# Chunk mask as extra contraction rows of the scores, attention output with queries on partitions, feed-forward transposed and spread between head pairs

## The chip, the cores and the metric

The kernel runs on one core of one Trainium2 chip. The metric is the device time of one execution in microseconds (us); the median of several runs is quoted.

Five engines work side by side, each on its own queue of instructions (in the kernel before TensorE is busy for 77% of the span and VectorE for 74%): TensorE (PE in the profile; PEld is its weight load), VectorE (DVE), ScalarE (ACT), GpSimd (POOL) and SyncE (SP). A matmul has a stationary operand (`lhsT`, loaded as weights: the page counts 2292 loads for the 2292 matmuls) and a moving one (`rhs`). Its cost is counted below in *columns* of the moving operand.

## The reference

Attention in which a query sees only its best 6 chunks of 32 keys, then a gated feed-forward. B=4, H=8, S=768, D=64; the feed-forward has width 512, and two halves of 512.

```python
k_min, k_max = k_chunks.min(axis=3), k_chunks.max(axis=3)             # per chunk of 32 keys
ub = sum(max(q * k_min, q * k_max), axis=-1)                          # bound of each chunk
top_chunks = argsort(where(causal_by_chunk, ub, -1e9))[..., -6:]
scores = where(chunk_selected & causal, q @ k.T / sqrt(D), -1e9)
x = softmax(scores) @ v                                               # heads side by side: B, S, 512
h = relu(x @ w_in); u, v = h[..., :512], h[..., 512:]
gated = u * (w_spatial @ layernorm(v) + b_spatial)                    # w_spatial mixes positions
out = gated @ w_out
```

## The kernel before

For each batch, for each of four head pairs: bounds and chunk selection (`sel_phase`), then scores and attention output (`score_phase`). After the four pairs, the feed-forward of that batch. The parts that matter (cuts marked with `...`):

```python
def score_phase(hi):
    ho = hi * D
    for gi, (q0, q1) in enumerate(qg_bounds):            # queries 0..511, 512..767
        av_ps = pst2([D + 1, 512])                       # head dim on partitions, plus the row of sums
        ...
        for t in range(t_last + 1):                      # key tiles of 128
            sc_ps = psum.tile([P, 512], F32, tag="sc", name="sc", bufs=2)
            mm(sc_ps[:, :Wv], lhsT=kT[ho:ho + D, t * P:(t + 1) * P],           # 64 rows
               rhs=qT[ho:ho + D, q0 + qoff:q1], start=True, stop=False)
            mm(sc_ps[:, :Wv], lhsT=expandM[:, t * P:(t + 1) * P],              # 24 rows: chunk mask
               rhs=selT[hi][:, q0 + qoff:q1], start=False, stop=True)
            if q0 + qoff <= t * P < q1:
                nc.vector.tensor_add(sc_ps[:, d0:d0 + P], sc_ps[:, d0:d0 + P], diagT)
            nc.scalar.activation(out=exp16[:, :Wv], in_=sc_ps[:, :Wv], func=Act.Exp, scale=scale)
            ...
        for t in range(t_last + 1):
            mm(av_ps[:, qoff:qoff + Wv], lhsT=v16[:, t, hi, :], rhs=exp16L[t][:, :Wv],   # 128 rows
               start=(t == 0), stop=(t == t_last))
        nc.vector.reciprocal(recip[:, :W], av_ps[D:D + 1, :W])                 # one partition, 512 columns
        nc.gpsimd.partition_broadcast(recip_bc_t[:, :W], recip[:, :W])
        nc.vector.tensor_mul(...)                                              # into xT
```

The weights, with the spatial matrix and its 36 transposes, are loaded before the first pair. The inputs come as float32 and are cast by ScalarE.

The softmax here doesn't subtract the row's maximum and nothing guards it: scores larger than these inputs give would overflow.

## Time and profile before

| | before |
|---|---|
| median | 689.34 us (687.81 to 690.26, 4 runs) |
| TensorE / VectorE / ScalarE busy | 529.4 / 508.3 / 224.2 us |
| one head pair | 31.3 us (mask matmuls of two neighbouring pairs start at 239.1 and 270.4 us) |

The page's first two parts, of the kernel before: busy time of each engine with its share of the span, and the span in 40 slices (tenths of busy; PEclk is the clock granted to TensorE in tenths).

```profile
PE 529.4 (77%) x2292; PEld 206.6 (30%) x2292; DVE 508.3 (74%) x1653; ACT 224.2 (33%) x464; POOL 50.2 (7%) x90
...
PE   0179797789778787969796877877976889796977
...
DVE  0177787877887778777977778786787877787686
...
PEclk9999999999885555555896555555688555555599
```

Neither TensorE nor VectorE is full, and neither has an idle stage. The clock is at half (5) in the attention of the second to fourth batch. The 9s of the first ten slices are not a measurement: the first record of the clock in this trace comes at 168.2 us, and what precedes it is shown as 1.0 (and counts as 1.0 in every mean clock quoted below, unless the text says that it is corrected). That TensorE was at half speed there too is seen from the spacing of its matmuls, in the timeline of the kernel before (start in us, duration in us, engine, line, operation, output and inputs, `partitions x elements`):

```profile
52.28 0.42 PE L195 MATMUL aps_454<-exp_471,v_253 128*65 128x256 f16 x1
52.63 0.39 PE L182 MATMUL sc<-qT,kT 64*128 64x256 f16 x1
52.95 0.39 PE L184 MATMUL sc<-selT_300,expandM 24*128 24x256 f16 x1
53.28 0.32 PE L195 MATMUL aps_454<-exp_477,v_253 128*65 128x128 f16 x1
...
58.04 0.42 PE L195 MATMUL aps_488<-exp_507,v_253 128*65 128x256 f16 x1
58.25 0.42 PE L195 MATMUL aps_488<-exp_513,v_253 128*65 128x256 f16 x1
...
172.22 0.38 PE L222 MATMUL sc<-w_in_sb,xT 128*128 128x512 f16 x1
172.44 0.38 PE L223 MATMUL aps_1772<-w_in_sb,xT 128*128 128x512 f16 x1
```

Read starts, not durations: durations overlap. Two attention-value matmuls of 256 columns start 0.21 us apart (58.04, 58.25); two feed-forward matmuls of 512 columns start 0.22 apart (172.22, 172.44). So the attention runs at half the rate per column. And L182 to L184, also 256 columns, takes 0.32: there is a gap of 0.11 us where the contraction goes from 64 rows to 24, and another where it goes on to 128. The records of the weight loads (PEld) fit a load that is not hidden: the loads of L182 and L184 start with their own matmuls (at 52.63 and 52.95 us, each 0.10 us long), while between the feed-forward matmuls, all of 128 rows, the load starts one matmul ahead (at 172.22 us for the matmul of 172.44).

The reciprocal of one row of 512 sums takes 3.35 us, and a diagonal mask add stands in the queue behind such a reciprocal. (This add then waited for its own matmul as well. Elsewhere the reciprocal alone holds it: one runs from 260.17 to 263.52 us, the matmul of the add behind it ends at 263.02, and the add starts at 263.56.) In the list of what each line waits for, the exponentials (L190) show the consequence: in all they waited 236.9 us for those adds (columns: releaser, us in total, times).

```profile
  DVE sc L188: 236.9, 134
  PE sc L184: 54.8, 99
```

The chain that ended last, kernel before:

```profile
PE 62%; DVE 22%; ACT 5%; issue 5%; DMA 3%; POOL 3%; DVEq 0%; POOLq 0%; ACTq 0%; SPq 0%
```

### The profile page before, as it was taken

How to read it: one execution, taken by the hardware profiler on the slowest of the kernel's cores; microseconds unless marked ns; L12 is line 12 of the kernel's file. 1: busy time of each engine (PE TensorE's matmuls, PEld its weight loads, DVE VectorE, ACT ScalarE, POOL GpSimd, SP SyncE). 2: the span in 40 equal slices, each digit the busy share in tenths (PEclk: the TensorE clock that was granted, in tenths of full speed). 3: DMA queues.
4: the chain of work that ended last, by engine and by line, in shares of the span. 5: the costliest groups of instructions: out<-in, count | busy, mean ns of one | idle time of the engine just before them, and what ended most of it. 6: DMA issues, size and time to landing. Idle time of an engine off the chain costs nothing.

```text
span 688.0 us, 7728 instructions
## 1 busy us (share of the span) xinstructions
PE 529.4 (77%) x2292; PEld 206.6 (30%) x2292; DVE 508.3 (74%) x1653; ACT 224.2 (33%) x464; POOL 50.2 (7%) x90
## 2 busy tenths in 40 slices
PE   0179797789778787969796877877976889796977
PEld 0133333223333233323333232322333333332333
DVE  0177787877887778777977778786787877787686
ACT  3135262423125233433205434343202524251310
POOL 4000010101000100001000101010000000010100
PEclk9999999999885555555896555555688555555599
DMA  9992121201041121210123110000001000000002
GB/s 198 209 211 47 30 46 44 58 2 30 0 139 32 44 46 30 46 30 0 29 77 82 26 29 23 7 7 0 7 22 71 0 7 1 7 0 6 5 2 93
DMA packets 83162, 29.99 MB, mean 44 GB/s; under 512 B 76208, under 2 KB 79536, under 8 KB 83120
## 3 DMA queue, kind: packets, MB, share of 16 engines
q1 hardware_dynamic: 81280, 26.75, 17.2%
q0 software_dynamic: 1840, 2.75, 2.2%
q8 instruction: 18, 0.29, 0.2%
q14 instruction: 24, 0.20, 0.1%
HBM read 24.38 MB, written 6.29 MB: 45 GB/s over the span
## 4 chain that ended last, share of the span: by engine, by line
PE 62%; DVE 22%; ACT 5%; issue 5%; DMA 3%; POOL 3%; DVEq 0%; POOLq 0%; ACTq 0%; SPq 0%
PE sc L184 15%; PE sc L182 12%; PE sc L245 5%; DVE selb L162 4%; DVE recip L198 4%; PE sc L222 3%; DMA ws_raw<-in_moe_w_spatial_dram 2%; POOL recip_bc_t L200 2%; DVE av_tmp L206 2%; PE aps L149 1%; DVE sc L188 1%; DVE ub_sb L152 1%; DVE stats L230 1%; PE aps L125 1%; PE aps L253 1%
## 5 line engine op out<-in xcount | busy, mean ns | idle before, releaser
L182 PE MATMUL sc<-qT,kT 64*128 64x256 f16 (+1 forms) x320 | 124.0, 396 | 28.6 <-ACT exp_1653 L190 1.4
L188 DVE TENSOR_TENSOR sc<-sc,diagT 128x128 f32<-128x128 f32 x192 | 53.8, 295 | 59.4 <-PE sc L184 47.6
L200 POOL PARTITION_BROADCAST recip_bc_t<-recip x64 | 43.0, 672 | 593.3 <-DVE recip L198 576.0
L167 PE MATMUL aps<-identity,selb 128*24 128x128 f16 x192 | 35.8, 276 | 44.5 <-DVE selb L162 39.6
L245 PE MATMUL sc<-vn_sb,wsT 128*128 128x512 f16 x144 | 47.4, 447 | 14.6 <-DVE vn_sb L239 14.6
L184 PEld LDWEIGHTS <-expandM 24*128 24x128 f16 x320 | 32.0, 100 | 88.1 <-issue 77.5
L182 PEld LDWEIGHTS <-kT 64*128 64x128 f16 x320 | 30.8, 100 | 87.2 <-issue 82.4
L222 PE MATMUL sc<-w_in_sb,xT 128*128 128x512 f16 x96 | 38.7, 440 | 0.0
L149 PE MATMUL aps<-kmaxP,qposF 64*128 64x24 f16 x192 | 22.1, 185 | 19.3 <-DVE ub_sb L152 12.5
L167 PEld LDWEIGHTS <-selb 128*24 128x24 f16 x192 | 17.9, 94 | 57.6 <-DVE selb L162 46.1
L97 PE MATMUL aps<-identity,ws_raw 128*128 128x128 f16 x36 | 5.3, 269 | 31.4 <-DMA ws_raw<-in_moe_w_spatial_dram 31.4
L98 DVE COPY wsT<-aps 128x128 f16<-128x128 f16 x36 | 5.3, 219 | 30.6 <-PE aps L97 30.6
L144 ACT ACTIVATE qposF<-qT 64x768 f16<-64x768 f16 x32 | 26.8, 836 | 0.4
L145 ACT ACTIVATE qnegNF<-qT 64x768 f16<-64x768 f16 x32 | 26.6, 831 | 0.2
L245 PEld LDWEIGHTS <-wsT 128*128 128x128 f16 x144 | 15.5, 109 | 34.4 <-issue 26.3
L149 PEld LDWEIGHTS <-qposF 64*128 64x128 f16 x192 | 14.1, 103 | 38.2 <-issue 29.3
L255 DVE COPY gT_sb<-aps 128x128 f16<-128x128 f16 x96 | 18.9, 218 | 7.9 <-PE aps L253 3.6
L234 ACT ACTIVATE rstd<-mv,eps_t 128x1 f32<-128x1 f32 x24 | 7.1, 294 | 52.4 <-DVE mv L232 52.4
L248 DVE SCALAR_TENSOR_TENSOR gated<-sc,u_sb 128x512 f16<-128x512 f32 x24 | 16.2, 688 | 10.1 <-PE sc L245 9.8
L150 PE MATMUL aps<-kminN,qnegNF 64*128 64x24 f16 x192 | 20.6, 178 | 1.8 <-ACT qnegNF L145 1.8
L126 DVE COPY qT<-aps 128x128 f16<-128x128 f16 x96 | 20.4, 212 | 1.9 <-PE aps L125 1.8
L123 DVE COPY kT<-aps 128x128 f16<-128x128 f16 x96 | 20.4, 213 | 0.1
(1506 smaller groups left out, 1150.7 us busy)
## 6 DMA issues: line engine op xcount, KB each, us to landing
out_dram<-out_sb SPq DMA_DIRECT2D x24, 256.0 KB, 2.0
ws_raw<-in_moe_w_spatial_dram POOLq DMA_DIRECT2D x1, 1152.0 KB, 16.2
w_in_sb<-in_moe_w_in_dram POOLq DMA_DIRECT2D x1, 1024.0 KB, 9.4
xT<-av_tmp SPq DMA_DIRECT2D x16, 64.0 KB, 1.9
w_out_sb<-in_moe_w_out_dram POOLq DMA_DIRECT2D x1, 512.0 KB, 10.9
xT<-av_tmp SPq DMA_DIRECT2D x16, 32.0 KB, 1.8
kp_242<-in_k_dram SPq DMA_DIRECT2D x2, 192.0 KB, 3.1
qp_243<-in_q_dram SPq DMA_DIRECT2D x2, 192.0 KB, 3.5
```

Of the source, the lines that this page charges most:

```text
L144: nc.scalar.activation(qpos, qT_h, func=Act.Relu)
L145: nc.scalar.activation(qnegN, qT_h, func=Act.Relu, scale=-1.0)
L149: mm(ub_ps, lhsT=qpos[:, qi * P:(qi + 1) * P], rhs=kmax, start=True, stop=False)
L162: nc.vector.tensor_scalar(selb, in0=ub_sbL[qi], scalar1=max8L[qi][:, TOPK - 1:TOPK], scalar2=NEG, op0=Alu.is_lt, op1=Alu.mult)
L167: nc.tensor.transpose(stp, selbL[qi], identity)
L182: mm(sc_ps[:, :Wv], lhsT=kT[ho:ho + D, t * P:(t + 1) * P], rhs=qT[ho:ho + D, q0 + qoff:q1], start=True, stop=False)
L184: mm(sc_ps[:, :Wv], lhsT=expandM[:, t * P:(t + 1) * P], rhs=selT[hi][:, q0 + qoff:q1], start=False, stop=True)
L188: nc.vector.tensor_add(sc_ps[:, d0:d0 + P], sc_ps[:, d0:d0 + P], diagT)
L198: nc.vector.reciprocal(recip[:, :W], av_ps[D:D + 1, :W])
L200: nc.gpsimd.partition_broadcast(recip_bc_t[:, :W], recip[:, :W])
L222: mm(hu, lhsT=lhsT, rhs=w_in_sb[:, ko, 0:DH], start=(ko == 0), stop=(ko == NDO - 1))
L245: mm(vs_ps, lhsT=wsT[:, si, ti * P:(ti + 1) * P], rhs=vn_sb[:, si, :], start=(si == 0), stop=(si == NQT - 1))
```

## The change

The intent: (1) put the chunk mask into the same matmul as the scores, by giving keys and queries 64 more rows that hold chunk membership and the selection flags, so that every contraction has 128 rows and the separate mask matmuls go; (2) compute the attention output with queries on partitions, so that the sums are a column and six reciprocals per partition suffice; (3) do the diagonal mask as a matmul of an identity with a triangle; (4) transpose six tiles into one PSUM tile and move them out with one instruction of 768 columns; (5) cast in the loads, issued by GpSimd; (6) compute the feed-forward transposed where that saves transposes, and place its pieces between the head pairs of the next batch.

The core of the diff (most of it cut):

```diff
-                        mm(sc_ps[:, :Wv], lhsT=kT[ho:ho + D, t * P:(t + 1) * P], rhs=qT[ho:ho + D, q0 + qoff:q1],
-                           start=True, stop=False)
-                        mm(sc_ps[:, :Wv], lhsT=expandM[:, t * P:(t + 1) * P], rhs=selT[hi][:, q0 + qoff:q1],
-                           start=False, stop=True)
-                        if q0 + qoff <= t * P < q1:
-                            nc.vector.tensor_add(sc_ps[:, d0:d0 + P], sc_ps[:, d0:d0 + P], diagT)
+                    mm(sc[:, col:col + n], lhsT=kh[hi][:, t * P:(t + 1) * P], rhs=a[hi][:, q0:q0 + n],
+                       start=True, stop=not dg)                       # 128 rows: 64 data, 64 mask
+                    if dg:
+                        mm(sc[:, col:col + P], lhsT=identity, rhs=tri, start=False, stop=True)
...
-                        mm(av_ps[:, qoff:qoff + Wv], lhsT=v16[:, t, hi, :], rhs=exp16L[t][:, :Wv], ...)
-                    nc.vector.reciprocal(recip[:, :W], av_ps[D:D + 1, :W])
-                    nc.gpsimd.partition_broadcast(recip_bc_t[:, :W], recip[:, :W])
+                    mm(avv[:, qi, :], lhsT=e[:, c:c + P], rhs=vt[:, t, hi, 0:D + 1],
+                       start=(t == 0), stop=(t == qi))
+            nc.vector.reciprocal(rec, avv[:, :, D:D + 1])             # 128 partitions, 6 columns
...
+            nc.gpsimd.tensor_tensor(km[:, m], in0=kmm[:, m:m + 1, :]..., in1=hmask..., op=Alu.mult)
...
+    load(0); load(1); load_weights(); prep(0)                         # (four lines)
+    for i in range(NPAIR):
+        if i + 2 < NPAIR: load(i + 2)
+        if i + 1 < NPAIR: prep(i + 1)
+        attend(i)
+        if i == 1: prep_weights()
+        ...                                                           # after the 4th pair: todo = mlp(b);
+            todo.pop(0)()                                             # else a share of the pieces
```

## The prediction

> **What bounds it now.** No engine is full: the page's busy shares are TensorE 77%, VectorE 74%, ScalarE 33%. The chain of waits is 62% TensorE, 22% VectorE, with the two score matmuls (queries times keys, then mask expansion) 27% of the span. The attention of a head pair takes about 31 us, the feed-forward of a batch about 36 us (group start times), in series; the first 36.5 us wait for the spatial weights.
>
> TensorE is slow there for two reasons, read in the timeline. A 256-column score matmul starts 0.325 us after the one before it, while attention-value matmuls of that width follow each other at 0.213: contraction rows switch between 64, 24 and 128, and each switch exposes about 0.11 us of weight load. And 0.213 us for 256 columns is half speed: feed-forward matmuls of 512 columns run at 0.216. The clock reads 0.50 in the attention after 202 us; the 1.00 before 178 us precedes the first record, and the spacings there contradict it. [...]
>
> **What changes.** Columns streamed per pair fall from 19,776 to 13,962 (mask matmuls and mask transposes go; attention-value 65 columns wide with 128 rows stationary; diagonal mask as an identity matmul added). Feed-forward stays at 58,368 per batch. In all 461,000 columns: 192 us at the fast clock, 385 at the slow. Every matmul has 128 contraction rows, so I expect loads hidden.
>
> VectorE (estimates from durations of before): per pair two reductions 1.9 us, two clamps 1.5, ten max 0.9, mask arithmetic 0.5, three 768-wide copies 2.5 (128-wide copies start 0.133 apart), normalisation 1.3: about 8.7. The 1x512 reciprocals (3.35 us each), the 192 diagonal adds (54 us) and small copies go. Feed-forward about 12.5 per batch. Sum about 195 against 508. ScalarE: exponentials of 1024 columns about 1.0 us; about 155 in all. GpSimd: 96 casting loads at about 1 us (weight loads: 0.8 to 1.06).
>
> **On the critical path.** Start: GpSimd is free at 9.4 us (as before), builds masks, first keys land near 22 us, scores near 33. Four pairs without feed-forward at about 13 us: 52. Twelve pairs with a quarter of a feed-forward each: TensorE 11.9 us fast, VectorE 12, ScalarE 10, coupled by two-deep PSUM buffers: about 16.5 each, 198. The last feed-forward stands alone: about 29. Sum about 312 us.
>
> **Predicted: 312 us, 8 in 10 between 268 and 372.** Faster by over 2%: 0.98; within 2%: 0.01; slower: 0.01.
>
> **What would show it.** First transposes near 22 us; granted clock mostly 1.0 in the middle, mixed in the first four pairs; score matmuls of 512 columns spaced near 0.22 us without load gaps; VectorE near 195 us busy; no engine over 85%; final stage of about 29 us with VectorE and ScalarE partly idle.
>
> **What would make it wrong.** If half clock holds through the middle, TensorE needs 24 us a pair and the time is near 400. If the two accumulator banks, shared by bounds, attention-value and feed-forward, make TensorE wait in order, pairs take 20 us (about 355). If the 128-byte casting loads land late, or the key-bound product on GpSimd queues behind loads, every pair waits. If all overlap well, pairs take 13.5 and the time is 270.

The kernel before shows this much: its feed-forward matmuls of 512 columns start 0.427 us apart from 163.8 us on and 0.216 us apart from 168.8 us on, after 5 us of them without a pause. So the full clock in the middle was the author's estimate. 33 to the first scores, 52 for four pairs, 198 for twelve and 29 for the end make 312 us. The landing of the first keys at 22 us and the first scores at 33 are estimates too, of which only GpSimd's start at 9.4 us was measured (9.35 in the kernel before). ScalarE's 1.0 us for 1024 columns is an estimate near what 0.485 us for 384 and 0.597 for 512 in the kernel before give (1.04). The first record of the clock, of 1.0, starts at 168.2 us and ends at 178.4; the prediction's 178 is its end.

## More of the kernel before

VectorE timeline, kernel before:

```profile
247.71 3.35 DVE L198 RECIPROCAL recip<-aps_2641 1x512 f32<-1x512 f32 x1 [0.94 <-PE aps_2641 L195]
251.49 0.30 DVE L188 TENSOR_TENSOR sc<-sc,diagT 128x128 f32<-128x128 f32 x1 [0.43 <-PE sc L184]
```

## The result, and the profile after

| | before | after |
|---|---|---|
| median | 689.34 us (4 runs) | 290.94 us (289.23 to 292.39, 4 runs) |
| ratio of fast runs | | 0.422 (95% interval 0.4203 to 0.4236) |
| TensorE / VectorE / ScalarE busy, us | 529.4 / 508.3 / 224.2 | 222.4 / 170.7 / 154.3 |

Ratios are the mean time of one kernel's fast runs over that of the other's fast runs of the same rounds, so they are not quite the ratio of the medians. Executions over 1.5% slower than the fastest of the same kernel are left out of the means.

Page, kernel after, first two parts:

```profile
PE 222.4 (77%) x2340; PEld 144.9 (50%) x2340; DVE 170.7 (59%) x498; ACT 154.3 (54%) x217; POOL 98.1 (34%) x150
...
PE   0037028787879798989798989978888989799994
...
DVE  8337005888788875565579865474688654238330
...
PEclk9999758999999999999999999999999999999999
```

The busy share of TensorE is 77% as before, and says nothing by itself: by the shapes in the traces it streamed 554,496 columns in 529.4 us busy before, 1.0 per ns, and now 461,472 in 222.4, 2.1 per ns. The clock is 1.0 from about 46 us to the end. TensorE stands still from about 29 to 40 us (fifth and sixth slice); we come back to that.

Timeline of TensorE, kernel after:

```profile
68.49 0.38 PE L213 MATMUL sc<-a_693,kh_0_92 128*128 128x512 f16 x1
68.70 0.22 PE L216 MATMUL sc<-tri,identity 128*128 128x128 f16 x1
68.76 0.38 PE L213 MATMUL sc<-a_693,kh_0_92 128*128 128x512 f16 x1
```

512 columns now take 0.21 us and the diagonal 0.06, with no gap although the stationary operand changes each time: the load of the next one starts with the matmul before it (the identity's at 68.49 us for 68.70, that of `kh` at 68.70 for 68.76).

Busy time by stage, kernel after: pairs without feed-forward (57 to 87 us), and two stretches of 60 us with it. Columns are the stretch, its length, then busy time and instructions of PE, PEld, DVE, ACT, POOL, then the clock, the DMA share and GB/s.

```profile
57.00:87.00 30.00, 24.56 (x373) 18.67 (x372) 24.51 (x78) 20.84 (x25) 18.00 (x27) 1.00 1.02 66
93.00:153.00 60.00, 52.87 (x573) 34.44 (x572) 38.88 (x117) 38.51 (x55) 21.31 (x32) 1.00 0.70 67
153.00:213.00 60.00, 53.39 (x577) 34.64 (x575) 39.60 (x119) 38.06 (x55) 18.89 (x28) 1.00 0.60 61
```

With feed-forward TensorE is busy 88 to 89%, VectorE about 65%. Without it TensorE and VectorE are level at 82%. The chain that ended last:

```profile
PE 50%; ACT 23%; DMA 8%; POOL 7%; DVE 7%; issue 3%; ACTq 0%; DVEq 0%; POOLq 0%
```

VectorE, 22% of the chain before, has fallen to 7%. ScalarE has risen from 5 to 23%, over half of it (13%) the exponentials: TensorE heads the chain, but ScalarE comes next, not VectorE.

### The profile page after: what moved, and what is told of

The parts are those of the page before. It is cut to its first block, busy times and chain, and to the rows that moved or that the text cites. A ratio compares the mean times of both kernels' runs of the same rounds, so it can differ in the third digit from the quotient of the medians.

```text
span 287.5 us, 5812 instructions
## 1 busy us (share of the span) xinstructions
PE 222.4 (77%) x2340; PEld 144.9 (50%) x2340; DVE 170.7 (59%) x498; ACT 154.3 (54%) x217; POOL 98.1 (34%) x150
## 4 chain that ended last, share of the span: by engine, by line
PE 50%; ACT 23%; DMA 8%; POOL 7%; DVE 7%; issue 3%; ACTq 0%; DVEq 0%; POOLq 0%
ACT e L217 13%; PE acc L322 11%; PE sc L213 7%; PE acc L310 7%; DMA w_out_sb<-in_moe_w_out_dram 6%; PE acc L224 5%; PE acc L333 5%; PE acc L285 5%; DVE stats L289 2%; PE tr L234 2%; POOL kp L140 2%; PE sc L216 2%; DMA out_dram<-o 2%; ACT uT L312 2%; PE acc L324 2%
## 5 line engine op out<-in xcount | busy, mean ns | idle before, releaser
L217 ACT ACTIVATE e<-sc 128x1024 f16<-128x1024 f32 (+1 forms) x96 | 84.0, 916 | 44.0 <-PE sc L216 42.9
L140 POOL DMA_DIRECT2D kp<-in_k_dram x32 | 26.7, 839 | 54.1 <-PE tr L152 48.0
L224 PEld LDWEIGHTS <-e 128*128 128x128 f16 x672 | 27.0, 98 | 31.3 <-ACT e L217 17.8
L216 PE MATMUL sc<-tri,identity 128*128 128x128 f16 x192 | 39.5, 222 | 0.0
L322 PE MATMUL acc<-wsT,vn 128*128 128x512 f16 (+1 forms) x192 | 37.2, 325 | 0.4 <-ACT uT L312 0.2
L322 PEld LDWEIGHTS <-vn 128*128 128x128 f16 x192 | 18.2, 98 | 12.2 <-issue 1.1
L310 PE MATMUL acc<-xT,w_in_sb 128*128 128x512 f16 (+1 forms) x128 | 23.4, 325 | 0.9 <-ACT uT L312 0.7
L333 PE MATMUL acc<-w_out_sb,gT 128*128 128x512 f16 x96 | 23.1, 378 | 0.4 <-ACT o L336 0.3
L216 PEld LDWEIGHTS <-identity 128*128 128x128 f16 x192 | 19.0, 99 | 7.4 <-issue 5.7
L285 PE MATMUL acc<-w_in_sb,xT 128*128 128x512 f16 x96 | 22.2, 379 | 0.0
L152 PE MATMUL tr<-identity,kp 128*128 128x128 f16 x96 | 10.0, 229 | 14.7 <-DMA kp<-in_k_dram 14.6
L180 DVE TENSOR_TENSOR acc<-acc,cmask 128x40 f32<-128x40 f32 x16 | 3.3, 208 | 25.6 <-PE acc L177 22.7
L161 POOL TENSOR_TENSOR km<-kmm,hmask 128x48 f16<-128x48 f16 x32 | 8.3, 276 | 26.3 <-DVE kmm L155 22.6
```

The lines of the kernel that those rows point to most:

```text
L140: nc.gpsimd.dma_start(out=kp[:, :, hi, :], in_=view(k))
L216: mm(sc[:, col:col + P], lhsT=identity, rhs=tri, start=False, stop=True)
L217: nc.scalar.activation(out=e[:, BASES[g]:BASES[g] + WIDTHS[g]], in_=sc[:, 0:WIDTHS[g]], func=Act.Exp, scale=scale)
L224: mm(avv[:, qi, :], lhsT=e[:, c:c + P], rhs=vt[:, t, hi, 0:D + 1], start=(t == 0), stop=(t == qi))
L285: mm(hv, lhsT=x[:, ko, bi * P:(bi + 1) * P], rhs=w_in_sb[:, ko, DH:DFF], start=(ko == 0), stop=(ko == NDO - 1))
L310: mm(hu[:, 0:t1 - t0], lhsT=w_in_sb[:, ko, db * P:(db + 1) * P], rhs=x[:, ko, t0:t1], start=(ko == 0), stop=(ko == NDO - 1))
```

## The experiments

Twelve kernels were run, in four groups; those of a group ran on the same chip. The first asks what each part of the change is worth, from the changed kernel; the second loosens one limit at a time in the kernel before; the third (b_both, km_late, best) and the fourth (mask_group2) follow what these pointed to.

### 1. Feed-forward not spread (nospread)

```diff
             todo = mlp(b)
+            while todo:
+                todo.pop(0)()
```

> The changed kernel, but the feed-forward of a batch is run whole after its fourth head pair, not spread over the next four. Theory A (spreading only fills gaps of TensorE, which stays at the fast clock either way): a pair alone takes 8.7 us as in the first batch, a feed-forward alone about 33 us as at the end, so a batch takes about 68 us where it took 60: about 315 us in all (305 to 325), clock near 1.0. Theory B (the spread matmuls are what keeps the clock fast): the attention falls back to clock 0.5, a pair takes 12 us or more, and the time is over 360 us.

Measured: 292.55 us median (ratio to before 0.4248, interval 0.4226 to 0.427), against 290.94 and 0.4203 to 0.4236 with the spread. The clock stayed at 1.0. Both theories missed. TensorE's busy time in two stretches of this kernel shows why:

```profile
105.00:120.00 15.00, 12.17 (x190) 8.99 (x188) 9.84 (x39) 10.06 (x14) 7.49 (x11) 1.00 0.98 136
...
150.00:165.00 15.00, 14.97 (x90) 8.38 (x88) 6.08 (x12) 4.40 (x9) 0.00 (x0) 1.00 0.03 9
```

Attention alone (first stretch) fills TensorE to 81%, and the feed-forward with some scores of the next pair (second) now fills it to 100%: together the same average as in the mixed order. The estimate of 33 us for a feed-forward alone was taken from the end of the program, where nothing else is left to fill in. In the middle the scheduler still mixes the instructions of a whole feed-forward with those of the next pair. The order of the pieces in the source was worth nothing measurable; this experiment does not make the feed-forward strictly serial, so it does not say what a strict order would cost.

### 2. The mask split off again (mask_split), and its control (mask_zero)

```diff
-  mm(sc[..], lhsT=kh[hi][:, tile], rhs=a[hi][:, q0:q0 + n], start=True, stop=not dg)
+  kr, mr = (D, 0) if hi == 0 else (0, D)
+  mm(sc[..], lhsT=kh[hi][kr:kr + D, tile], rhs=a[hi][kr:kr + D, q0:q0 + n], start=True, stop=False)
+  mm(sc[..], lhsT=kh[hi][mr:mr + NCH, tile], rhs=a[hi][mr:mr + NCH, q0:q0 + n], start=False, stop=not dg)
```

> The changed kernel, but each score strip as two matmuls from the same tiles: 64 rows of queries and keys, then the 24 mask rows. Adds 86,016 columns, 36 us at the fast clock. If only columns count: about 325 us, the same as the next run. If a switch of the number of contraction rows also exposes weight load (0.05 to 0.11 us each, some 500 to 800 switches): 355 to 400 us, with gaps between these matmuls that the next run does not have.

The control:

```diff
+  mm(sc[..], lhsT=kh[hi][:, tile], rhs=a[hi][:, q0:q0 + n], start=True, stop=False)
+  mm(sc[..], lhsT=zeros, rhs=a[hi][:, q0:q0 + n], start=False, stop=not dg)      # 128 rows of zeros
```

> Control for the run before: as many matmuls and columns, but the first keeps all 128 rows with mask, and the second multiplies by a 128-row tile of zeros, so rows never switch. Expected about 325 us (315 to 330) under every theory; matmuls of 512 columns 0.216 us apart.

Measured: the control 314.57 us (ratio 0.4571), 24 us over the changed kernel, less than the 36 us of its columns, as some of them fell into idle time. The split kernel took 468.96 us in its one fast run (mean clock 0.817; its other three runs, 478.19 to 479.81, count as slow): 154 us more than the control for the same matmuls and columns. (No interval can be given for one run, but 154 us is far beyond the 11 us between its runs.) That is beyond the expected range of 355 to 400.

The timelines of the two, at the same place of the program. Split (profile of a slow run; the clock is 1.0 at this point):

```profile
152.45 0.39 PE L214 MATMUL sc<-a,kh 64*128 64x512 f16 x1
152.77 0.39 PE L216 MATMUL sc<-a,kh 24*128 24x512 f16 x1
153.09 0.23 PE L219 MATMUL sc<-tri,identity 128*128 128x128 f16 x1
153.25 0.33 PE L214 MATMUL sc<-a,kh 64*128 64x384 f16 x1
```

Control:

```profile
151.09 0.38 PE L215 MATMUL sc<-a,kh 128*128 128x512 f16 x1
151.30 0.38 PE L217 MATMUL sc<-a,zeros 128*128 128x512 f16 x1
151.52 0.22 PE L220 MATMUL sc<-tri,identity 128*128 128x128 f16 x1
151.57 0.33 PE L215 MATMUL sc<-a,kh 128*128 128x384 f16 x1
```

512 columns take 0.32 us in the split kernel and 0.21 in the control: every change of the number of rows costs about 0.11 us. As in the kernel before, the weight load starts with its own matmul there (at 152.76 and 153.08 us, 0.09 and 0.10 us long). The instruction order has 759 such changes, so about 81 us (an estimate: 759 times 0.107). The rest goes with the clock. The mean of the profiled run, 0.796, is too high: its first record comes at 145.3 us, and until then the spacing is that of half speed (256 columns of 64 rows start 0.32 us apart at 61.87 and 62.19 us, 0.21 of it streaming). With that stretch as half, the clock is 0.64, and 0.93 in the control. Worked out from the trace so, the half clock costs the split kernel 117 us of streaming more than the control, and the gaps 84; 37 us of the two fell into time in which the control's TensorE was idle, which leaves the 164 us between the two profiled spans. All this although TensorE is recorded busy 92% of the span: the record counts each matmul's whole duration (0.39 us for starts 0.32 apart), gaps included. So the clock did not fall for want of recorded busy time; experiment 7 comes back to what it fell for.

### 3. Before with 128-row score matmuls (b_rows)

The kernel before, same columns; the query tile of each head is zero in the other head's rows, and mask and selection tiles are padded with zero rows.

```diff
-  lhsT=kT[ho:ho + D, t * P:(t + 1) * P], rhs=qT[ho:ho + D, q0 + qoff:q1]
+  lhsT=kT[:, t * P:(t + 1) * P], rhs=qTh[hi][:, q0 + qoff:q1]
-  expandM = cp.tile([NCH, S], F16)
+  expandM = cp.tile([P, S], F16)             # and selT the same, zeroed by GpSimd
```

> The kernel before, same columns, but the two score matmuls of every tile contract over 128 rows (zeros below the mask rows, zeros in the other head's query rows), as the attention-value matmuls do. Theory A (switching rows exposes about 0.107 us of weight load each time, and partial rows keep the clock at half): score matmuls of 256 columns follow each other without the 0.11 us gap, some 100 us of gaps go, and if the clock rises, up to 130 us more, until VectorE (508 us busy, now some 10 more) limits: about 590 us (540 to 640). Theory B (before was limited by VectorE and its chain): over 655 us.

Measured: 673.21 us, ratio 0.9767 (0.9733 to 0.98). The gaps went, as this timeline of the kernel shows, here while the clock was at 1.0:

```profile
242.99 0.27 PE L188 MATMUL sc<-qTh,kT 128*128 128x256 f16 x1
243.10 0.27 PE L190 MATMUL sc<-selT,expandM 128*128 128x256 f16 x1
243.21 0.27 PE L201 MATMUL aps<-exp,v 128*65 128x256 f16 x1
```

And TensorE needs 410.6 us busy in place of 529.4, with the clock often up in the attention (mean 0.69 in place of 0.59, both corrected for the stretch before the first record). But the time hardly moved; theory A was wrong about the size, and the time lies in theory B's range. The edit is not free: it adds 24 us to VectorE (508.3 to 532.5, the query tiles are copied per head) and 45 us to GpSimd, so 16 us is, if anything, less than the rows were worth. The page's busy line and its chain:

```profile
PE 410.6 (61%) x2292; PEld 223.2 (33%) x2292; DVE 532.5 (79%) x1749; ACT 219.4 (33%) x464; POOL 95.3 (14%) x154
...
DVE 37%; PE 36%; issue 10%; ACT 8%; POOL 6%; DMA 4%; POOLq 0%; ACTq 0%; DVEq 0%
DVE recip L204 11%; PE sc L190 6%; PE aps L201 6%; PE sc L188 6%; PE sc L251 5%; ACT exp L196 5%; DVE selb L168 4%; PE aps L262 3%; POOL recip_bc_t L206 3%; DMA ws_raw<-in_moe_w_spatial_dram 2%; DVE max L163 2%; PE aps L229 2%; DVE selT L174 2%; PE sc L228 2%; DVE sc L194 2%
```

VectorE, 22% of the chain before, is now level with TensorE (37 and 36%), with the reciprocals at its head.

### 4. Before with a lighter VectorE (b_norecip, b_lightdve)

```diff
-  nc.vector.reciprocal(recip[:, :W], av_ps[D:D + 1, :W])
+  nc.vector.tensor_copy(recip[:, :W], av_ps[D:D + 1, :W])       # both; wrong result on purpose
-  nc.vector.tensor_add(sc_ps[:, d0:d0 + P], sc_ps[:, d0:d0 + P], diagT)
+  pass                                                          # b_lightdve only
```

> The kernel before with the 64 one-row reciprocals replaced by plain copies (wrong result on purpose): takes some 140 us of busy time off VectorE. Theory A (TensorE's rows and clock limit): 645 to 675 us, a few per cent, as the reciprocal is 3.5% of the chain. Theory B (VectorE limits, its queue holds back the diagonal adds): under 600 us.

> As the run before, and the 192 diagonal adds of VectorE left out too (wrong result on purpose): VectorE loses some 190 of 508 us. Theory A: 620 to 660 us. Theory B: under 560 us.

Measured: 632.09 us (ratio 0.9179) and 629.77 us (0.9146). The first lies between the two theories; the second in theory A's range. VectorE fell to 337.1 us busy in the second, and the time stopped at 630: TensorE, 82% busy and 75% of the chain there, held it. From the page of b_lightdve:

```profile
PE 518.1 (82%) x2292; PEld 205.4 (33%) x2292; DVE 337.1 (54%) x1461; ACT 229.7 (37%) x464; POOL 50.2 (8%) x90
...
PE 75%; DVE 16%; issue 3%; DMA 3%; ACT 1%; POOL 1%; POOLq 0%; ACTq 0%
```

### 5. Both together (b_both)

> The kernel before with both relaxations together: 128-row score matmuls, and neither the one-row reciprocals nor the diagonal adds (wrong result on purpose). If before had two limits side by side, TensorE's gaps and clock and VectorE's queue, each hiding the other, the two together give far more than their sum: 430 to 540 us, and the clock mostly 1.0 in the attention. If the gains only add (16 and 59 us): about 614 us.

Measured: 509.4 us, ratio 0.7402 (0.7383 to 0.7421). Alone, the two loosenings gave 16 and 59 us; together they gave 180. The page of this kernel:

```profile
PE 364.0 (72%) x2292; PEld 195.1 (38%) x2292; DVE 364.1 (72%) x1557; ACT 220.6 (44%) x464; POOL 93.6 (18%) x154
...
PEclk9999859679997779789988679788989588787989
```

This is the main finding on the kernel before: two limits stood side by side, TensorE's row changes with its half clock, and VectorE's one-row reciprocals and diagonal adds. Taking one away left the other. The change took both. What carries on from 509 to 291 us (fewer columns, fewer and wider evictions, no serial feed-forward, an earlier start) was not separated by a run.

### 6. Before with useless matmuls (b_fill)

```diff
+  for _ in range(2):
+      mm(fill_ps[:, :Wv], lhsT=identity, rhs=exp16[:, :Wv], start=True, stop=True)   # after each exponential
```

(One of the four small PSUM buffers was given up for the output.)

> The kernel before with two more, useless, 128-row matmuls after each exponential (10,752 columns a pair, 54% more). If the half clock came from too little dense work, the clock in the attention goes to 0.9 or more and the time changes by less than 10% (620 to 760 us) in spite of the extra work; if the clock is low for another reason it stays near 0.5 and the time goes over 780 us.

Measured: 818.11 us, ratio 1.1877, with the clock in the attention unchanged:

```profile
PE 666.0 (82%) x2932; PEld 280.4 (34%) x2932; DVE 513.4 (63%) x1653; ACT 227.0 (28%) x464; POOL 50.2 (6%) x90
...
PEclk9999999999995555555795555555598555555589
```

Two more matmuls after each exponential did not raise the clock, while in b_rows the same work without row changes, at a lower busy share (61% against 82%), did (0.66 in place of 0.50 from 239 to 271 us). So too little *recorded* busy time is not the reason for the half clock. The row changes were as many as before (937, before 981); how much of the array was really at work is taken up in the next experiment.

### 7. Row changes or partial rows (mask_group2)

The split kernel of experiment 2, reordered: up to two 64-row matmuls, then two 24-row ones, then the diagonals.

> The split-mask kernel (64 rows, then 24 rows) with the same matmuls and columns, but ordered so that up to two 64-row matmuls, then two 24-row ones, then the diagonals follow each other: by the instruction order TensorE's row count changes 532 times in place of 759. At 0.107 us each that is 24 us less: 445 to 455 us if nothing else changes. If the gaps are what pulls the clock down, the clock rises clearly over the 0.75 to 0.82 of the split kernel and the time goes below 430 us; if the partly filled rows themselves pull it down, the clock stays at 0.75 to 0.82.

Measured: 419.03 us (ratio 0.6086), mean clock 0.827 to 0.839, against 468.96 us and 0.817 in the split kernel's fast run. The gain of 50 us is twice the 24 us of the gaps saved. The means hide the rise of the clock, as they count the stretch before the first record as 1.0 (98.3 us here, 145.3 in the profiled split run): corrected, the clock rose from 0.64 to 0.72. So fewer gaps do raise it. The run also shows that a gap belongs to the change and not to the partly filled rows, here at the full clock:

```profile
329.89 0.59 PE L216 MATMUL sc<-a,kh 64*128 64x512 f16 x2
330.42 0.60 PE L219 MATMUL sc<-a,kh 24*128 24x512 f16 x1
```

From the start of the two matmuls of 64 rows and 512 columns to that of the 24-row one are about 0.52 us: twice 0.21, and one gap of about 0.1 at the end.

Whether the gaps or the partly filled rows lower the clock, no run separates. A count over the kept traces, made after the runs, says that both do. The clock's records last multiples of 3.41 us in these traces (in the kernel before 3.413, 6.827, 10.24, 13.653, 17.067, 20.48 and 126.293 us: 1 to 6 and 37 times 3.413), so each trace was cut at their edges into windows of that length. In each window the time in which columns streamed was added up (0.417 ns a column at the full clock, where 128 and 512 columns start 0.056 and 0.215 us apart in the kernel after; 0.833 at half, where they start 0.107 and 0.427 apart in the kernel before), each matmul weighted with its rows over 128: a share of filled rows. Of 826 windows at the full clock in all fourteen traces, the clock fell after each of the 108 with a share of 0.354 or less, and after none of the 718 with 0.362 or more. Of 741 at half clock, it rose after those above about 0.75, with 6 exceptions. Without the weight for rows, the best limits leave 22 and 40 exceptions. (With it, the two kernels' own traces, before and after, alone give: from full, it fell after 9 windows with shares up to 0.32 and held after 97 with 0.38 or more; from half, it rose after 8 with 0.88 or more and stayed after 113 with 0.73 or less.) In the attention of b_fill (245 to 394 us) no window came above 0.71, in that of the kernel before (206 to 325 us) none above 0.52. Two windows, of the split kernel and of the changed one, each with the next (columns as above, PE's busy time second):

```profile
152.14:155.55 3.41, 3.41 (x17) 1.49 (x16) 3.12 (x6) 2.05 (x2) 2.05 (x4) 1.00 0.90 61
155.55:158.96 3.41, 3.41 (x29) 1.69 (x28) 0.99 (x11) 2.48 (x4) 0.00 (x0) 0.50 0.02 1
...
62.76:66.17 3.41, 1.82 (x43) 1.54 (x40) 2.88 (x9) 3.00 (x4) 2.07 (x4) 1.00 0.89 60
66.17:69.58 3.41, 2.52 (x40) 1.75 (x40) 3.19 (x15) 0.50 (x2) 2.43 (x3) 1.00 0.49 31
```

The split kernel is recorded busy all of the first window, but its share of filled rows is 0.22 (the timeline in experiment 2 lies in it), and the clock falls. The changed kernel is recorded busy 53% of its window, with a share of 0.38, and keeps the full clock. The limits were found in the same traces that they describe; no run was made to test them.

### 8. The early stall (km_dve, km_late)

In the changed kernel TensorE stands still early. Its list of waits (engine, line, what it waited for, total us, times, longest):

```profile
PE acc L177 <- POOL km L161: 14.5, 4, 11.0
```

L161 is the small product of key bounds on GpSimd; in GpSimd's queue it stood behind loads that waited until the big weight loads had landed (loads of `vt`, `kp` and `qs` at 28.88, 35.13 and 37.28 us, after waits of 3.48, 5.43 and 1.32 us for `w_in_sb`, `ws_raw` and `w_out_sb`; the product ran at 39.74). The edit of km_dve is one word, `nc.gpsimd.tensor_tensor(km...)` to `nc.vector.tensor_tensor(km...)`.

> The changed kernel, but the key-bound product (two small multiplies a pair) is on VectorE, not GpSimd. Theory: TensorE stood still from 29 to 40 us because this product was in GpSimd's queue behind loads that waited for the weights; so about 11 us less: 280 us (277 to 284), and nothing changes later. Rival: the loads themselves were late; then the stall stays under another name and the time is 288 to 292 us.

Measured: 283.84 us, ratio 0.4116 (0.4105 to 0.4127). Seven of the 11 us came, at the upper end of the first range. The rest appears under another name, in the timeline of TensorE:

```profile
39.23 0.82 PE L152 MATMUL tr<-identity,kp 128*128 128x128 f16 x6 [5.49 <-DMA kp<-in_k_dram]
```

The third pair's keys themselves waited behind the weights. So the loads were late as well, as the rival said. km_late also moves the weight loads behind the fourth pair's inputs, and the spatial transposes one pair later:

> The changed kernel with the key-bound product on VectorE (as in the run before that gave 283.8 us) and the feed-forward weights loaded after the fourth pair's inputs. If the rest of the early stall (5.5 us of TensorE waiting for the third pair's keys behind the weights) goes: 277 to 280 us. If the weights now hold up later loads by as much: 282 to 286 us.

Measured: 276.94 us (275.03 to 279.12, 5 runs), ratio 0.4016 (0.3996 to 0.4036).

### 9. Diagonal mask off TensorE (best)

```diff
-  if dg:
-      mm(sc[:, col:col + P], lhsT=identity, rhs=tri, start=False, stop=True)
+  # after the exponential: e[diagonal block] *= triangle of ones and zeros, on VectorE
+  nc.vector.tensor_tensor(two, in0=two, in1=tri.unsqueeze(1).to_broadcast([P, 2, P]), op=Alu.mult)
```

> As the run before, with the keys of both heads loaded first, and the diagonal mask as a multiplication of the exponentials on VectorE in place of 192 identity matmuls. If TensorE limits the stages with feed-forward (88 to 93% busy), 24,576 columns less are worth up to 10 us: 267 to 272 us. If VectorE's extra step between exponential and attention-value matmul delays TensorE as much, no better than the run before.

Measured: 273.34 us (272.09 to 273.37), ratio 0.3963 (0.3955 to 0.3972): correct, and faster than both kernels, 6% under the changed one (273.34 against 290.94, in separate rounds). The step itself, with the new order of the first loads, gave 3.6 us of the up to 10 expected, between the two cases. VectorE is now 72% busy and TensorE 79%, and VectorE's share of the chain went from 13% in km_late to 21%: the extra step on VectorE probably took back part of it, which no run shows by itself. The run does not separate the load order from the mask.

## Why the prediction was right, point by point

The time, 291 us, lies in the range of 268 to 372, 7% under the 312 predicted. Pairs are counted from 0. The stages, with the transposes of each pair's output as marks:

| | predicted | measured |
|---|---|---|
| scores of the first pair | 33 | 25.6, but then the stall; the second head's scores at 42.7 |
| end of pair 3 | 85 | 78.2 |
| end of pair 15 | 283 (198 for 12 pairs) | 253.1 (175) |
| end | 312 (29 more) | 287.5 in the profiled run (34 more) |

- **What bounded before.** Row changes with exposed weight load: right; 0.11 us each, shown by the split kernel against its control. Half clock in the attention: right. But "TensorE is slow there for two reasons" missed that VectorE held the time just as firmly. Experiments 3 to 5 show it: with the row changes of the scores gone and part of the clock back, the time fell by 16 us only.
- **The cause of the half clock.** The prediction expected the full clock from dense work. The feed-forward of the kernel before agrees with that (0.427 us per 512 columns, and 0.216 after 5 us of it). The attention does not, if dense is what the profile records as busy: at 82% (b_fill) and 92% (split) recorded busy it stayed at or fell to half. It does if dense is the share of filled rows counted in experiment 7. The outcome was predicted rightly (1.0 in the middle), and every contraction of 128 rows was part of the plan for another reason, to hide the loads: that it also kept the clock up was not foreseen.
- **VectorE 195 us.** Measured 170.7. The mis-sized term: "three 768-wide copies 2.5". They took 0.55 us each, 1.7 in all, and start 0.48 apart. The estimate scaled up copies of 128 columns, 0.133 apart, as if all of that were per column. Measured, 768 columns in 0.48 us are 1.6 columns per ns, and 128 in 0.133 are 1.0. The clamps of 640 columns were over-estimated the same way (0.48 in place of 0.75). Ten max took 0.91 us as predicted, and ScalarE's total is 154.3 against "about 155".
- **Pairs.** "About 13 us" without feed-forward was too much: 8.7 (output transposes at 69.5, 78.2, 86.9). The sum of VectorE's work was the right measure, and the margin for coupling too big. That the first four pairs still took the 52 us predicted (25.6 to 78.2 us, 52.6) is luck: the stall until 40 us, the half clock until 46 us and the transposes of the spatial matrix came in these pairs and took about what they saved. With feed-forward "about 16.5 each": 15.0 (60 us for four pairs). The prediction had TensorE and VectorE level there (11.9 and 12 us a pair); measured, TensorE is ahead, 88% busy against 65%. Most of the 7% between prediction and result lies here: 175 us in place of 198 for twelve pairs.
- **Start.** First keys at 14.6 us, not 22, but the listed risk that the key-bound product "queues behind loads" came true once, and cost 11 us of TensorE's time; removing it by km_dve and km_late took the time to 277.
- **End.** 34 us, not 29: the previous batch's last pieces were still in the queue when the last pair ended.
- **The spread.** The prediction costed a quarter of a feed-forward beside each pair. The spread itself was not what paid: without it the time is the same.

## What to carry to other kernels

Give matmuls that follow each other the same number of contraction rows, padding with zeros if need be: here (kernel before, half clock) 256 columns of 24 rows took 0.32 us with the gap of a row change and 256 columns of 128 rows 0.21 without one, so fewer rows saved nothing and the change cost 0.11 us. In these traces the clock followed the share of rows that were filled and streaming, not the recorded busy time (at full clock it fell after shares up to 0.354 and held from 0.362). When two engines are each about three quarters busy with no idle stage, suspect two limits that hide each other: 16 and 59 us alone became 180 together, so try the removals jointly before you dismiss one. And keep small steps of the critical path out of a queue that also issues loads.

## What else the traces show

- Weight loads were hidden between matmuls with the same 128 rows (kernel after, 512 columns 0.215 us apart with new weights each time), and exposed where the row count changed: by 0.11 us from 64 rows to 24 and from 24 to 128 (256 columns 0.32 us apart in the kernel before), by 0.14 from 128 to 64 (0.356 apart); in the split kernel by 0.11 (512 columns 0.32 us apart).
- Runs of transposes in the kernel after took 0.219 us each and started 0.055 us apart (six in 0.51 us) at clock 1.0. Whether transposes alone would raise the clock, no run here shows.
- The reciprocal took 3.35 us for 1x512 and 1.75 us for 1x256 in the kernel before, that is 6.2 ns for each further column, and 0.19 us for 128x6 in the kernel after.
- The granted clock in a profile reads 1.0 before its first record (168.2 us into the kernel before), where the matmul spacing shows half speed.
